# One packed array of per-partition constants in a retention, expert and feed-forward kernel

## The chip, the cores and the metric

The kernel runs on 1 core of one Trainium2 chip. Its time is device microseconds of one execution, the median over a few runs. The core's engines are TensorE (PE, its weight load PEld), VectorE (DVE), ScalarE (ACT), GpSimd (POOL) and SyncE (SP); a "q" behind an engine's name (SPq, ACTq) is its queue of DMA issues.

## The reference

Three layers follow each other. First a retention attention over 2 batches, 8 heads, 768 tokens and 64 features, in blocks, with a decay `lam` per head; then a mixture of 8 experts, one per token, chosen by gate logits with a bias that depends on the token's modality; then a feed-forward layer of width 2048.

```python
Dmask = np.where(rel >= 0, lam[:, None, None] ** rel[None, :, :], 0.0)
lam_pow = lam[:, None, None] ** (pos[None, :, None] + 1)
for b in range(nb):
    intra = np.einsum('bhic,bhjc->bhij', qb, kb) * Dmask[None]
    intra = np.einsum('bhij,bhjd->bhid', intra, vb)
    inter = np.einsum('bhid,bhde->bhie', qb * lam_pow[None], kv_state)
    out[:, :, sl] = intra + inter
    kv_state = lam_block * kv_state + np.einsum('bhsd,bhse->bhde', kb * rev_pow[None], vb)
...
logits = x @ w_gate + modality_bias[modality_id]
e_idx = np.argmax(logits, axis=1)
out[mask] = gate_w[mask, None] * (np.maximum(x[mask] @ w1[e], 0.0) @ w2[e])
...
h = x @ w_in
return (h * np.clip(h + 3.0, 0.0, 6.0) / 6.0) @ w_out
```

## The kernel before, in words

The work has three stages in time: the attention (to about 75 us), the experts (to about 230 us) and the feed-forward layer (to the end). The attention goes over 12 units of 128 tokens, alternating between the two batches. Each unit has four loads of 256 KB: q_t and k_t (`load`, L326) and k_n and v_n (`load_rows`, L336). The tiles have four buffers, so units 0 to 2 are loaded up front and unit u+3 in the loop.

Before the loads of units 0 and 1 are finished, small constants are loaded:

- `lam_bc` (L350): the 8 decays, the same on every partition, 32 bytes per partition, from ACT.
- `lam_p` (L353): for each of the two halves of the partitions, every second decay (4 numbers, with a step of 2 in memory), in two transfers from ACT.
- the gate columns (L360): `w_gate`, four runs of 8 numbers per partition, straight into the last 8 columns of `iw`, whose first 128 columns of each block are the identity; from SP.
- `bias_bc` (L362): the 16 modality biases on every partition; from SP.
- `mod_i` (L366): the modality of each token; from SP.

What uses them: DVE makes `dmask` from `lam_bc` with eight scans (L373), and in `late_constants` (L398) `qdec` from `lam_p` with four scans (L400), `m_f` from `mod_i` (L408), and `bias_tok` from `m_f` and `bias_bc` (L413 to L416). The matmuls of `rows` (L539, tile `xr`) multiply with `iw`, and so transpose a unit and compute its logits.

PE, ACT, DVE and SP run in the order in which the code is written; POOL's order is left to a scheduler. The order at the start is: 36 warm-up matmuls that use no input (L698, tile `warm`), `scores(0)` with its two mask products on DVE (L449, L451, tile `s_t`), `late_constants`, `decays(0)` on POOL and `key_decays(0)` on ACT (L459, L478, tile `k_d`), then for each unit the scores and mask products of the next unit, the state products (L499, tile `s_ps`) and the output products (L519, tile `o_ps`) of this one, and the `xr` matmuls of the unit before. So on DVE the mask products of unit 1 stand behind `qdec`, `m_f` and `bias_tok`. The second scores tile of unit 1 lies in the PSUM bank `xa` (L444), which the first `xr` tile (L537) uses next.

Each DMA from SP or ACT reports to one of eight semaphores (DMAHW0 to DMAHW7), in turn; a transfer waits until the one that used its semaphore eight transfers earlier has landed.

Of the kernel before, what the change touches and what calls it, by code (L numbers as in the profile page):

```python
# [11 lines left out]
F32 = mybir.dt.float32  # L12
# [11 lines left out]
P = 128  # L24
B, H, S, D = 2, 8, 768, 64
KA = 4
NPAIR = H // 2
# [5 lines left out]
KD = DM // P  # L33
E = 8
# [18 lines left out]


@with_exitstack
def retention_moe_ffn(ctx, tc, qT, kT, kn, vn, lam, mod, w_gate, bias, w1, w2, win, wout, out):
    nc = tc.nc
    ctx.enter_context(tc.manual_schedule(engines={ENG.PE, ENG.Activation, ENG.DVE, ENG.SP}))

# [253 lines left out]
    with ExitStack() as ac:  # L313
        acon = ac.enter_context(tc.tile_pool(name="acon", bufs=1))
# [11 lines left out]
        def load(u):  # L326
            b, c = units[u]
            i = b * NC + c
            q_t = ap.tile([P, NPAIR, C], F32, tag="q_t", name="q_t")
            k_t = ap.tile([P, NPAIR, C], F32, tag="k_t", name="k_t")  # L330
            v_n = ap.tile([P, DM], F32, tag="v_n", name="v_n")
            nc.sync.dma_start(out=q_t, in_=qT[i])
            nc.sync.dma_start(out=k_t, in_=kT[i])
            data[u] = (q_t, k_t, None, v_n)

        def load_rows(u):  # L336
            b, c = units[u]
            i = b * NC + c
            q_t, k_t, _, v_n = data[u]
            k_n = None  # L340
            if c < NC - 1:
                k_n = ap.tile([P, H, D], F32, tag="k_n", name="k_n")
                nc.sync.dma_start(out=k_n, in_=kn[i])
            nc.sync.dma_start(out=v_n, in_=vn[i])
            data[u] = (q_t, k_t, k_n, v_n)

        load(0)
        load(1)
        lam_bc = acon.tile([P, H], F32, name="lam_bc")
        nc.scalar.dma_start(out=lam_bc, in_=lam[0:1, :].broadcast_to([P, H]))  # L350
        lam_p = acon.tile([P, NPAIR], F32, name="lam_p")
        for t in range(2):
            nc.scalar.dma_start(  # L353
                out=lam_p[t * D:(t + 1) * D, :],
                in_=lam.rearrange("o (p t) -> o t p", t=2)[:, t, :].broadcast_to([D, NPAIR]),
            )
        load_rows(0)
        load_rows(1)
        iw = acon.tile([P, KD, P + E], F32, name="iw")
        nc.sync.dma_start(out=iw[:, :, P:], in_=w_gate.rearrange("(k p) e -> p k e", p=P))  # L360
        bias_bc = acon.tile([P, 2, E], F32, name="bias_bc")
        nc.sync.dma_start(  # L362
            out=bias_bc.rearrange("p m e -> p (m e)"),
            in_=bias.rearrange("m e -> (m e)").unsqueeze(0).broadcast_to([P, 2 * E]))
        mod_i = acon.tile([P, NTILE], I64, name="mod_i")
        nc.sync.dma_start(out=mod_i, in_=mod)  # L366

# [2 lines left out]
        for t in range(2):  # L370
            for p in range(NPAIR):
                h = 2 * p + t
                nc.vector.tensor_tensor_scan(  # L373
                    out=dmask[:, h, :], data0=lam_bc[:, h:h + 1].broadcast_to([P, C]), data1=ident,
# [12 lines left out]
            out=tri_bf, in_=ones_bf, pattern=[[1, P]], base=0, channel_multiplier=-1,  # L387
# [4 lines left out]
        iota(off_e, [[NT, E]])  # L392
        for k in range(KD):
            nc.gpsimd.tensor_copy(iw[:, k, :P], ident)
        qdec = acon.tile([P, NPAIR, C], F32, name="qdec")
        bias_tok = acon.tile([P, NC, B, E], F32, name="bias_tok")

# [421 lines left out]
    def picked(first, out):  # L819
# [7 lines left out]
            out=gt, in0=nrest.unsqueeze(2).broadcast_to([P, E, JMAX]), in1=thr, op=ALU.is_gt),  # L827
# [24 lines left out]
            out=posf, in0=ohs, in1=sxo.unsqueeze(1).broadcast_to([P, NTILE, E]), op=ALU.mult),  # L852
# [5 lines left out]
            out=to_a, in0=a_io[:, :NTILE].unsqueeze(1).broadcast_to([P, NTILE, NTILE]),  # L858
            in1=pos_a.unsqueeze(2).broadcast_to([P, NTILE, NTILE]), op=ALU.is_equal),
        lambda: V.tensor_tensor(  # L860
            out=to_ao, in0=to_a,
            in1=o_num.rearrange("p c b -> p (c b)").unsqueeze(2).broadcast_to([P, NTILE, NTILE]), op=ALU.mult),
        lambda: V.tensor_tensor(
            out=at_b, in0=b_io.unsqueeze(1).broadcast_to([P, NTILE, P]),
# [40 lines left out]
    with ExitStack() as fc:  # L905
# [52 lines left out]
        for n, (fb, tg, f) in enumerate(steps):  # L958
            m = n % (NTG * FB)
# [17 lines left out]
        for h in range(2):  # L977
            nc.vector.tensor_scalar(  # L978
                out=row2[:, h:h + 1], in0=row[:, i:i + 1], scalar1=2, scalar2=h, op0=ALU.mult, op1=ALU.add)
        ts = slice(TG - P, TG)  # L980
        for h in range(2):
# [3 lines left out]
            for f in range(FB):  # L985
# [6 lines left out]
                out=out.rearrange("n (h c) -> (n h) c", h=2),  # L992
                out_offset=bass.IndirectOffsetOnAxis(ap=row2[:, h:h + 1], axis=0),
                in_=acc[:, i, cs], in_offset=None), "out")


def _layout(inputs):
    f = {k: np.asarray(v) for k, v in inputs.items()}

    def feature_major(a):  # L1000
        a = a.reshape(B, NPAIR, 2, NC, C, D).transpose(0, 3, 2, 5, 1, 4)
        return np.ascontiguousarray(a).reshape(B * NC, P, NPAIR, C)

    def token_major(a):
        return np.ascontiguousarray(a.transpose(0, 2, 1, 3)).reshape(B * NC, C, DM)

    w1 = f["moe_w1"].reshape(E, KD, P, KF1 // 2, 2, P).transpose(0, 3, 2, 4, 1, 5)
    w2 = f["moe_w2"].reshape(E, KF1, P, KD, P).transpose(0, 3, 2, 1, 4)
    win = f["moe2_w_in"].reshape(KD, P, NFB, FB, P).transpose(2, 1, 3, 0, 4)
    wout = f["moe2_w_out"].reshape(NFB, FB, P, DM).transpose(0, 2, 1, 3)  # L1010
    return {
        "qT": feature_major(f["q"]),
        "kT": feature_major(f["k"]),
        "kn": token_major(f["k"]).reshape(B * NC, C, H, D),
        "vn": token_major(f["v"]),
        "lam": f["lam"].reshape(1, H),
        "mod": np.ascontiguousarray(f["moe_modality_id"].reshape(B, NC, P).transpose(2, 1, 0)).reshape(P, NTILE),
        "w_gate": f["moe_w_gate"],
        "bias": f["moe_modality_bias"],
        "w1": np.ascontiguousarray(w1).reshape(E, KF1 // 2, P, 1024),  # L1020
        "w2": np.ascontiguousarray(w2).reshape(E, KD, P, 1024),
        "win": np.ascontiguousarray(win).reshape(NFB, P, FB * DM).view(np.int64),
        "wout": np.ascontiguousarray(wout).reshape(NFB, P, FB * DM).view(np.int64),
    }
# [17 lines left out]
```

## Time and profile before

| what | us |
|---|---|
| median of 3 runs | 507.0 |
| lowest and highest run | 506.35, 510.4 |
| profiled execution, its own time | 509.76 |
| its span, first to last instruction | 507.8 |
| PE busy in the span | 483.7 |
| DVE, ACT, POOL busy | 315.1, 219.5, 71.6 |
| mean granted TensorE clock | 0.98 of full |

Busy times are those of one profiled execution, and its times below are microseconds from the first instruction. PE is busy 95% of the span, so a gain has to come from the rest or from matmuls that run at a lower clock.

### The profile page before, as it was taken

The page shows a single profiled execution, that of the slowest core. Times are in us where ns is not written, and L with a number is a line of the kernel's source. Part 1 is how long each engine was busy: PE and PEld are TensorE (multiplying, and loading weights), DVE is VectorE, ACT ScalarE, POOL GpSimd, SP SyncE. Part 2 cuts the span into 40 slices and gives each one's busy share as a digit, 9 for nine tenths or more (in the row PEclk, how much of TensorE's full clock was granted, in tenths as well). Part 3 has the DMA queues.
Part 4 walks back from the last instruction along what each step waited for, and adds up shares of the span by engine and source line. Part 5 has one row for each costly group of instructions (what it writes and reads, how often), then busy time and mean ns, then how long its engine had stood idle before and what let it go on. Part 6 is the DMA issues. An engine that isn't in the chain of part 4 may idle for free.

```text
span 507.8 us, 8695 instructions
## 1 busy us (share of the span) xinstructions
PE 483.7 (95%) x3322; PEld 424.1 (84%) x3322; DVE 315.1 (62%) x615; ACT 219.5 (43%) x405; POOL 71.6 (14%) x106
## 2 busy tenths in 40 slices
PE   5999999889999999996999999999999999999995
PEld 4878789789999999995888888888888888888885
DVE  4577789856888877661647445766556776424252
ACT  0555556356666565631453534343334334222230
POOL 3554351320303030000000000000000000003033
PEclk8899999989999999997999999999999999999998
DMA  4986463866868776602212211221203120002022
GB/s 137 370 275 198 159 240 129 243 176 215 267 227 265 233 221 196 229 25 87 80 46 83 62 63 43 83 79 46 83 16 110 43 83 1 0 0 84 0 84 83
DMA packets 25327, 64.29 MB, mean 127 GB/s; under 512 B 5954, under 2 KB 6053, under 8 KB 25277
## 3 DMA queue, kind: packets, MB, share of 16 engines
q1 hardware_dynamic: 22173, 57.25, 35.1%
q0 software_dynamic: 2416, 6.39, 3.8%
q8 instruction: 28, 0.46, 0.4%
q14 instruction: 22, 0.18, 0.1%
q10 hardware_dynamic: 688, 0.01, 0.1%
HBM read 57.29 MB, written 6.34 MB: 125 GB/s over the span
## 4 chain that ended last, share of the span: by engine, by line
PE 53%; POOL 0%; POOLq 0%; DVE 0%; issue 0%
PE ph L925 27%; PE po L944 26%; POOLq L1038 0%; POOL out_y L991 0%; POOL out_y L953 0%; DVE acc L951 0%; DVE row L978 0%
## 5 line engine op out<-in xcount | busy, mean ns | idle before, releaser
L930 DVE SCALAR_TENSOR_TENSOR g<-r,ph 128x512 f32<-128x512 f32 x48 | 33.0, 687 | 68.1 <-ACT r L928 68.1
L944 PE MATMUL po<-wo_hi,g_lo 128*128 128x512 f32 x188 | 74.0, 394 | 0.0
L944 PE MATMUL po<-wo_lo,g_hi 128*128 128x512 f32 x188 | 73.9, 393 | 0.0
L944 PE MATMUL po<-wo_hi,g_hi 128*128 128x512 f32 x188 | 73.1, 389 | 0.0
L928 ACT ACTIVATE r<-ph,half 128x512 f32<-128x512 f32 x48 | 33.0, 688 | 81.3 <-PE ph L925 81.3
L214 DVE TENSOR_TENSOR wlo<-wraw,whi 128x1024 fp32r<-128x1024 f32 x46 | 56.1, 1222 | 16.7 <-ACT whi L210 16.6
L925 PE MATMUL ph<-y_hi,wi_hi 128*128 128x512 f32 x192 | 53.6, 402 | 4.0 <-DVEq L886 4.0
L953 POOL DMA_INDIRECT out_y<-acc,row x11 | 10.7, 968 | 307.5 <-DVE acc L951 304.5
L925 PE MATMUL ph<-y_lo,wi_hi 128*128 128x512 f32 x192 | 53.9, 403 | 0.0
L934 DVE TENSOR_TENSOR g_lo<-g,g_hi 128x512 fp32r<-128x512 f32 x48 | 33.3, 693 | 33.0 <-ACT g_hi L932 33.0
L925 PE MATMUL ph<-y_hi,wi_lo 128*128 128x512 f32 x192 | 53.2, 399 | 0.0
L210 ACT CAST whi<-wraw 128x1024 fp32r<-128x1024 f32 x48 | 50.1, 1046 | 4.4 <-DMA wraw<-in_w 4.4
L925 PEld LDWEIGHTS ph<-y_hi,wi_hi 128*128 128x128 f32 x192 | 36.9, 193 | 12.4 <-ACTq L886 4.2
L932 ACT CAST g_hi<-g 128x512 fp32r<-128x512 f32 x48 | 29.8, 621 | 36.2 <-DVE g L930 36.2
L925 PEld LDWEIGHTS ph<-y_hi,wi_lo 128*128 128x128 f32 x192 | 36.9, 192 | 8.8
L925 PEld LDWEIGHTS ph<-y_lo,wi_hi 128*128 128x128 f32 x192 | 36.6, 191 | 8.8
L944 PEld LDWEIGHTS po<-wo_lo,g_hi 128*128 128x128 f32 x188 | 35.3, 188 | 8.6
L944 PEld LDWEIGHTS po<-wo_hi,g_hi 128*128 128x128 f32 x188 | 35.4, 188 | 8.4
L944 PEld LDWEIGHTS po<-wo_hi,g_lo 128*128 128x128 f32 x188 | 35.3, 188 | 7.5
L226 POOL DMA_INDIRECT xg<-x_d,ix x18 | 23.0, 1277 | 89.1 <-DMA ix<-order_d 59.6
L273 PE MATMUL ps<-x_hi,whi 128*128 128x264 f32 x192 | 31.9, 289 | 0.0
L273 PE MATMUL ps<-x_lo,whi 128*128 128x264 f32 x192 | 31.7, 288 | 0.0
(173 smaller groups left out, 796.9 us busy)
## 6 DMA issues: line engine op xcount, KB each, us to landing
wraw<-in_w SPq DMA_DIRECT2D x48, 512.0 KB, 3.7
raw<-in_win SPq DMA_DIRECT2D x16, 512.0 KB, 3.8
raw<-in_wout SPq DMA_DIRECT2D x16, 512.0 KB, 4.8
q_t<-in_qT SPq DMA_DIRECT2D x12, 256.0 KB, 4.5
k_t<-in_kT SPq DMA_DIRECT2D x12, 256.0 KB, 4.9
v_n<-in_vn SPq DMA_DIRECT2D x12, 256.0 KB, 5.6
x_d<-x_s SPq DMA_DIRECT2D x12, 256.0 KB, 2.3
k_n<-in_kn SPq DMA_DIRECT2D x10, 256.0 KB, 7.8
```

The costliest lines, as they stand in the source:

```text
L210: nc.scalar.copy(hi.rearrange("p a f -> p (a f)"), raw)
L214: (low or nc.vector).tensor_tensor(out=lo[:, js, :], in0=raw.rearrange("p (a f) -> p a f", f=P)[:, js, :], in1=hi.bitcast(F32)[:, js, :], ...
L226: ld = nc.gpsimd.indirect_dma_start(out=xg, out_offset=None, in_=x_d[0:EARLY * B * P, :] if s == LEAD else x_d[:], in_offset=bass.Indirect ...
L273: nc.tensor.matmul(ps, w[:, 4 * f2 + k, :], x[:, k, :], start=(m == 0), stop=(m == 3 * KD - 1))
L925: nc.tensor.matmul(ph, w[:, f, k, :], y[:, k, cols], start=(n == 0), stop=(n == 3 * KD - 1))
L928: nc.scalar.activation(r6, ph, ACTF.Relu, scale=1.0 / 6.0, bias=half)
L930: nc.vector.scalar_tensor_tensor(out=g, in0=r6, scalar=1.0, in1=ph, op0=ALU.min, op1=ALU.mult)
L932: nc.scalar.copy(g_hi, g)
L934: nc.vector.tensor_tensor(out=g_lo, in0=g, in1=g_hi.bitcast(F32), op=ALU.subtract)
L944: nc.tensor.matmul(pos_[t], g[:, ts], w[:, f, :], start=(f == 0 and n == 0), stop=(f == FB - 1 and n == 2))
L953: rows_apart(nc.gpsimd.indirect_dma_start(out=out, out_offset=bass.IndirectOffsetOnAxis(ap=row[:, i:i + 1], axis=0), in_=acc[:, i, :], in_ ...
```

## The change

The host lays lam (8 columns), the per-half lam (4), the gate columns (32) and the two bias rows (16) out as one array of 128 rows with 60 numbers, 240 bytes each. One transfer from ACT, where `lam_bc` was, loads it into the tile `cst`; `lam_bc`, `lam_p`, `gate_c` and `bias_bc` are slices of that tile. The gate columns come into `iw` by a copy on POOL.

```diff
-def retention_moe_ffn(ctx, tc, qT, kT, kn, vn, lam, mod, w_gate, bias, w1, w2, win, wout, out):
+def retention_moe_ffn(ctx, tc, qT, kT, kn, vn, small, mod, w1, w2, win, wout, out):
...
-        lam_bc = acon.tile([P, H], F32, name="lam_bc")
-        nc.scalar.dma_start(out=lam_bc, in_=lam[0:1, :].broadcast_to([P, H]))
-        lam_p = acon.tile([P, NPAIR], F32, name="lam_p")
-        for t in range(2):
-            nc.scalar.dma_start(
-                out=lam_p[t * D:(t + 1) * D, :],
-                in_=lam.rearrange("o (p t) -> o t p", t=2)[:, t, :].broadcast_to([D, NPAIR]),
-            )
+
+        cst = acon.tile([P, H + NPAIR + KD * E + 2 * E], F32, name="cst")
+        nc.scalar.dma_start(out=cst, in_=small)
+        lam_bc = cst[:, :H]
+        lam_p = cst[:, H:H + NPAIR]
+        gate_c = cst[:, H + NPAIR:H + NPAIR + KD * E].rearrange("p (k e) -> p k e", k=KD)
+        bias_bc = cst[:, H + NPAIR + KD * E:].rearrange("p (m e) -> p m e", m=2)
         load_rows(0)
         load_rows(1)
         iw = acon.tile([P, KD, P + E], F32, name="iw")
-        nc.sync.dma_start(out=iw[:, :, P:], in_=w_gate.rearrange("(k p) e -> p k e", p=P))
-        bias_bc = acon.tile([P, 2, E], F32, name="bias_bc")
-        nc.sync.dma_start(
-            out=bias_bc.rearrange("p m e -> p (m e)"),
-            in_=bias.rearrange("m e -> (m e)").unsqueeze(0).broadcast_to([P, 2 * E]))
         mod_i = acon.tile([P, NTILE], I64, name="mod_i")
         nc.sync.dma_start(out=mod_i, in_=mod)
...
         for k in range(KD):
             nc.gpsimd.tensor_copy(iw[:, k, :P], ident)
+        nc.gpsimd.tensor_copy(iw[:, :, P:], gate_c)
...
+    lam, gate = f["lam"], f["moe_w_gate"]
+    small = np.concatenate([
+        np.broadcast_to(lam, (P, H)),
+        np.repeat(lam.reshape(NPAIR, 2).T, D, axis=0),
+        gate.reshape(KD, P, E).transpose(1, 0, 2).reshape(P, KD * E),
+        np.broadcast_to(f["moe_modality_bias"].reshape(1, 2 * E), (P, 2 * E)),
+    ], axis=1)
```

SP's queue at the start, before, from the fifth transfer on, with the semaphore that each waits for (DMAHW0 is that of lam_bc, DMAHW1 of the first q_t, DMAHW2 and DMAHW4 of the two lam_p):

```order
L343 DMA k_n_142<-in_kn 128x512
L344 DMA v_n_129<-in_vn 128x512 [waits DMAHW0_49]
L343 DMA k_n_145<-in_kn 128x512 [waits DMAHW1_49]
L344 DMA v_n_134<-in_vn 128x512 [waits DMAHW2_49]
L360 DMA iw_148<-in_w_gate 128x4x8 [waits DMAHW3_49]
L362 DMA bias_bc_150<-in_bias 128x16 [waits DMAHW4_49]
L366 DMA mod_i_152<-in_mod 128x12 [waits DMAHW5_49]
L332 DMA q_t_190<-in_qT 128x512 [waits DMAHW6_49]
L333 DMA k_t_191<-in_kT 128x512 [waits DMAHW7_49]
```

The same place now (DMAHW0 is that of cst, DMAHW1 and DMAHW2 of the first q_t and k_t):

```order
L343 DMA k_n_139<-in_kn 128x512
L344 DMA v_n_129<-in_vn 128x512
L343 DMA k_n_142<-in_kn 128x512
L344 DMA v_n_134<-in_vn 128x512 [waits DMAHW0_49]
L360 DMA mod_i_146<-in_mod 128x12 [waits DMAHW1_49]
L332 DMA q_t_185<-in_qT 128x512 [waits DMAHW2_49]
L333 DMA k_t_186<-in_kT 128x512 [waits DMAHW3_49]
```

Two transfers are gone from SP and two from ACT, the rest keeps its order; two transfers that waited now wait for nothing, and the others wait for other transfers than before.

POOL at the start, the difference between before (-) and now (+), around the copies into `iw`:

```order
 L74 IOTA rev_e 128x8
 L74 IOTA off_e 128x8
-L394 COPY iw<-ident 128x128 [waits Pool_49]
-L386 AFFINE_SELECT tri_bf<-ones_bf 128x128 [waits Pool_49]
-L394 COPY iw<-ident 128x128 x3
-L417 MEMSET half 128x1
+L388 COPY iw<-ident 128x128 [waits Pool_49]
+L380 AFFINE_SELECT tri_bf<-ones_bf 128x128 [waits Pool_49]
+L388 COPY iw<-ident 128x128 x3
+L389 COPY iw<-cst 128x4x8 [waits DMAHW0_49]
+L412 MEMSET half 128x1
 L74 IOTA thr 128x48
```

The copy of the gate columns, which waits for cst, stands in front of `half` and the iotas of `late_constants`; apart from line numbers nothing else moved on POOL. The order on PE and DVE is the one of before.

## Rows read from the trace of the kernel before

**Rows 1.** The page: PE's busy tenths in 40 slices of the span.
```profile
PE   5999999889999999996999999999999999999995
```

**Rows 2.** Timeline of PE: start, us, instructions, [idle before, releaser].
```profile
6.73 0.61 PE L449 MATMUL sc<-q_t,k_t 64*128 64x128 f32 x7
11.77 2.08 PE L449 MATMUL sc<-q_t,k_t 64*128 64x128 f32 x16 [4.43 <-DMA k_t<-in_kT]
...
15.49 1.71 PE L519 MATMUL o_ps<-s_t,v_n 128*64 128x128 f32 x15
17.13 1.16 PE L449 MATMUL sc<-q_t,k_t 64*128 64x128 f32 x16
18.22 0.50 PE L539 MATMUL xr<-iw,x_t 128*128 128x136 f32 x2
```

**Rows 3.** Timeline of DVE, 4 to 18.5 us.
```profile
4.66 2.65 DVE L373 TENSOR_TENSOR_SCAN dmask<-lam_bc,ident 128x128 f32<-128x128 f32 x8 [4.66 <-DMA lam_bc<-in_lam]
7.37 1.29 DVE L451 TENSOR_TENSOR s_t<-sc,dmask 128x512 f32<-128x512 f32 x2
11.25 1.37 DVE L400 TENSOR_TENSOR_SCAN qdec<-lam_p,zrow 128x128 f32<-128x128 f32 x4 [2.59 <-DMA lam_p<-in_lam]
15.20 0.25 DVE L408 TENSOR_SCALAR m_f<-mod_i 128x12 f32<-128x12 int32 x2 [2.58 <-DMA mod_i<-in_mod]
...
15.87 0.74 DVE L416 TENSOR_TENSOR bias_tok<-bias_tok,b 128x96 f32<-128x96 f32 x1
16.54 1.27 DVE L451 TENSOR_TENSOR s_t<-sc,dmask 128x512 f32<-128x512 f32 x2
```

**Rows 4.** Timeline of POOL and ACT, up to 15 us.
```profile
5.22 0.29 POOL L429 TENSOR_SCALAR_AFFINE_SELECT below<-below 128x64 f32<-128x64 f32 x1
...
12.38 1.28 ACT L478 ACT_TABLE_LOAD   x1 [12.38 <-DMA k_n<-in_kn]
12.46 0.62 POOL L459 TENSOR_TENSOR k_d<-k_n,dmask 128x256 f32<-128x256 f32 x1 [6.95 <-DMA k_n<-in_kn]
...
13.68 1.06 ACT L478 ACTIVATE k_d<-k_n,dmask 128x64 f32<-128x64 f32 x4
```

**Rows 5.** Windows: length, PE PEld DVE ACT POOL busy (count), clock, DMA share, GB/s.
```profile
2.00:5.00 3.00, 3.00 (x30) 3.00 (x29) 0.34 (x1) 0.00 (x0) 3.00 (x16) 1.00 0.62 169
5.00:8.00 3.00, 2.34 (x25) 1.95 (x22) 2.94 (x10) 0.00 (x0) 0.43 (x3) 1.00 0.27 88
8.00:10.00 2.00, 0.00 (x0) 0.00 (x0) 0.66 (x2) 0.00 (x0) 0.00 (x0) 1.00 0.06 13
...
10.30:11.00 0.70, 0.00 (x0) 0.00 (x0) 0.00 (x0) 0.00 (x0) 0.00 (x0) 0.50 0.89 310
11.00:16.00 5.00, 4.00 (x39) 3.74 (x41) 2.13 (x9) 2.35 (x5) 1.47 (x3) 0.50 1.07 352
```

**Rows 6.** Timeline of the DMA issues of ACT and SP: start, us of issue.
```profile
1.26 0.42 SPq L333 DMA_DIRECT2D k_t<-in_kT  x1
1.27 1.40 ACTq L353 DMA_DIRECT2D lam_p<-in_lam  x2
...
1.73 0.42 SPq L332 DMA_DIRECT2D q_t<-in_qT  x1
...
2.20 0.55 SPq L333 DMA_DIRECT2D k_t<-in_kT  x1
...
7.77 0.51 SPq L360 DMA_DIRECT2D iw<-in_w_gate  x1
11.17 0.34 SPq L362 DMA_DIRECT2D bias_bc<-in_bias  x1
```

**Rows 7.** DMA queue of ACT, first 16 us: packets, MB, share of 16 engines.
```profile
q10 hardware_dynamic: 688, 0.01, 2.0%
```

**Rows 8.** SP's waits: us in total, times, longest.
```profile
SPq L362 <- DMA lam_p<-in_lam: 2.9, 1, 2.9
```

**Rows 9.** Windows, 20 to 25 us.
```profile
20.00:25.00 5.00, 5.00 (x82) 4.40 (x80) 2.12 (x6) 2.32 (x7) 4.81 (x9) 1.00 1.05 383
```

More of the change, by code (lines that the diff above doesn't have):

```diff
@@ L1015, in _layout @@
         "vn": token_major(f["v"]),
-        "lam": f["lam"].reshape(1, H),
+        "small": small,
         "mod": np.ascontiguousarray(f["moe_modality_id"].reshape(B, NC, P).transpose(2, 1, 0)).reshape(P, NTILE),
-        "w_gate": f["moe_w_gate"],
-        "bias": f["moe_modality_bias"],
         "w1": np.ascontiguousarray(w1).reshape(E, KF1 // 2, P, 1024),
```

## Prediction

> **What bounds the kernel now.** I read the page first, for where TensorE is not busy. Its 40 slices of 12.7 us show PE at 8 to 9 tenths almost everywhere; the first stands at 5, the last at 5 too, and one near the middle, between the expert stage and the last stage, at 6 [rows 1]. All that the change touches is loaded once, in that first slice, so the question is what ends last there, and whether time won there lasts to the end of the program.
>
> Next, the engines in the order of time. In the first 17 us each of them waits for a DMA: PE for k_t of unit 1 (4.43 us, until 11.77), DVE for lam_p and then for mod, ACT and POOL for k_n until 12.4 [rows 2 to 4]. The transfers were not short of bandwidth: the core moved 169 GB/s from 2 to 5 us, 88 from 5 to 8, 13 from 8 to 10, and 352 from 11 to 16 us [rows 5]. The loads stood still while most of the first eight were issued.
>
> Bytes against issue order tell what they stood behind. A load of q_t, k_t, k_n or v_n is 256 KB, 0.262 MB. From 2 to 5 us came 0.507 MB, nearly q_t and k_t of unit 0; from 5 to 8 us 0.264 MB, one load, q_t of unit 1; then almost nothing, and from 10.3 us the rest pours in [rows 5]. After the first q_t and lam_bc, the issues were k_t at 1.26, two lam_p from 1.27 on over 1.40 us, q_t at 1.73, k_t at 2.20 [rows 6]. So the slow stretches lie just where a lam_p stands. Each lam_p reads one number at a time: ACT's queue made 688 packets for 0.01 MB, 640 of them data (128 for lam_bc, 256 for each lam_p), the rest 16 completions for each of three transfers [rows 7]. Moreover SP's bias_bc, which reuses the second lam_p's semaphore, waits for it 2.9 us, until 11.17, and behind it stand mod and all loads of unit 2 [rows 6, 8].
>
> **The change, part by part.**
>
> Removed: three ACT transfers become one, and w_gate (0.51 us of issue) and bias_bc (0.34) leave SP's queue [rows 6]. In the new order v_n of unit 0 and k_n of unit 1 wait for nothing, v_n of unit 1 for cst, mod for the first q_t. Everything up to mod can be issued by about 5.5 us instead of after 11.5.
>
> The new array has 128 rows of 240 bytes and takes lam_bc's place in front. The trace has no such transfer; nearest is lam_bc, 128 rows of 32 bytes, for which DVE waits until 4.66 [rows 3]. Earlier gains nothing: the first mask products start at 7.37, when the first scores end too (6.73 + 0.61 = 7.34) [rows 2, 3]. The other end is a landing as late as the second lam_p's, 11.25. I take 4.66, since form and place are lam_bc's.
>
> When do the loads land? With no lam_p between them the six left at 5 us are 1.57 MB; at the 383 GB/s of a busy stretch [rows 9] they end at 9.1 us. From bytes to release cost about 0.5: k_t and k_n, the first 0.524 MB after 10.3, were through at 11.9 (0.217 MB by 11.0, 0.307 MB at 352 GB/s), and ACT went on at 12.38 [rows 4, 5]. So k_t of unit 1 is there by 6.9, k_n of unit 0 by 7.6, mod by 9.7. These are late bounds, as bytes will flow better before 5 us too.
>
> The Trainium skill ("DMA: Bandwidth & Descriptors", Queues, rings and completion order) says that each DMA engine takes the queue rows that have work in turn, packet by packet, and that SP and ACT each have a row of their own. By that rule lam_p in ACT's row would not hold up the loads in SP's, the standstill would have another cause, and the sum would be the 0.9 us of the first rival instead of 5.4. The order of the bytes speaks against it so far.
>
> The DVE chain now: first mask products 7.37 to 8.66, qdec only at 11.25 (lam_p), m_f only at 15.20 (mod), second mask products at 16.54 [rows 3]. New: qdec at 8.66, needing only cst, plus 1.37 is 10.03; mod is there, and from m_f to the second products it takes 16.54 - 15.20 = 1.34, so they start at 11.37 and end 1.27 later, at 12.64. The start moves by 5.17 us.
>
> The PE chain: the scores of unit 1 follow those of unit 0 at 7.34. In the gap of now the granted clock fell, and it stood at 0.50, the 1.2 GHz level, over 11 to 16 us [rows 5]; the same 16 matmuls took 2.08 us there and 1.16 later [rows 2]. Without the gap I count full clock, and scores to 8.5. ACT: table load at 7.6, 1.28, so k_d begins at 8.9. From k_d's start to the end of the output products of unit 0 it took 13.68 to 17.20 [rows 2, 4], 3.5 us; by the ratio of the clock 2.0, so to 10.9, and the scores of unit 2 to 12.1. Next in PE's order are the xr matmuls, at 18.22 now. They write the bank that the second mask products have to leave: 12.64, say 12.8. That is 5.4 us earlier.
>
> From there PE's order is the same as before, and PE was busy 5.00 of 5.00 us from 20 to 25, with the loads already coming freely [rows 9]; no DMA of the first loads ends a wait behind it. So the shift goes through to the end. POOL gets a wait: the copy of the gate columns stands for cst in front of its iotas. That list ends at 5.51 now (5.22 + 0.29); with 1.5 us of wait and 0.3 for the copy it ends at 7.3, and POOL's next work, k_d, comes after k_n at 7.6, so the wait is covered. Its price without that cover is the 1.8 us, on POOL alone. Should the iotas slow the scans beside them by a tenth of 2.65 us, that is 0.3 us; I charge nothing, since they run beside them until 5.51 now too [rows 3, 4].
>
> **Sum.** 5.4 us off the profiled execution: span 507.8 to 502.4, its time 509.76 (1.96 around the span) to 504.4. The median of the runs is 507.0, 2.76 below the profiled one; on that footing the forecast is 501.6. Ends: 6.1 us if the last bias sum, 0.74 in the chain between m_f and the second products [rows 3], cost nothing; 0.9 if the standstill stays.
>
> **Rivals.**
>
> *The standstill has another cause, and the loads still come at 10.3.* For: the packets of ACT's queue filled only 2.0% of the engines' first 16 us [rows 7]. Against: the byte count, which stops twice in just that order. Then five loads (1.31 MB) stand before mod: 0.217 MB by 11.0, the rest at 383 GB/s to 13.9, landed 14.4, second products at 15.7, 0.9 us gained: 506.1. The Trainium skill (the same page, Rules for kernel authors) holds that a transfer issued early and waited for late has its fixed cost hidden, which would leave nothing to win by merging small ones but their issue. The trace does not agree here: DVE stood 2.59 us for lam_p and 2.58 for mod [rows 3].
>
> *Half of it returns.* mod lands late (each us past 10.03 costs one), or PE's clock falls again in the short waits around 8.7 and 12.4 us. Price of the clock: the work from 12.8 to about 17 at half speed, some 3 us. Against: the fall now came with 4.4 us without any matmul, and the new gaps are under 1 us. Gain 2.4: 504.6.
>
> *Slower: cst is late.* One transfer of 30 KB now gates the masks, which needed 4 KB. From its landing to the second mask products stand 2.65 + 1.29 + 1.37 + 1.34 = 6.65 us [rows 3], so it costs time from a landing at 16.54 - 6.65 = 9.89 on. At lam_p's 11.25 the products start at 17.9, 1.4 later: 508.4. For: it carries 7.5 times the bytes. Against: lam_bc, in the same number of rows, was there at 4.66.
>
> **How the numbers follow.** Forecast (4.5 to 6.1 us gained) 0.70; standstill stays 0.12; half returns 0.13; slower 0.05. A change of 1% is 5.07 us, about what a measurement of this kernel can tell from none; the forecast lies only just beyond it, so of its 0.70 I put 0.49 past 1%, and 0.01 on a larger gain elsewhere: faster 0.50. The rest of it, the two middle cases and part of the last are within 1%: 0.47; slower by over 1% 0.03. The range runs from a gain of 6.1 us, less twice the 0.65 between the two lower runs of before, to the case of the standstill: 499.6 to 506.1.
>
> **What would show it.** Right: no stretch of a microsecond under 100 GB/s between 3 and 9 us; second scores at about 7.4; qdec at 8.7, m_f by 10.1, second mask products near 11.4, xr near 12.8; granted clock at 1.00 through the first slice. Wrong: a standstill before 10 us without any lam_p; masks that begin later than 5 us; an early xr with a span that is not shorter.

## The result, and the profile after

| what | before | after |
|---|---|---|
| median of 20 executions, us | 508.64 | 501.12 |
| ratio, with its 95% interval | | 0.9875 (0.9856 to 0.9894) |
| profiled execution, its own time | 509.76 | 502.03 |
| its span | 507.8 | 500.2 |
| PE busy in the span | 483.7 | 480.8 |

The change makes the kernel 1.25% faster, 5.4 to 7.3 us of 508.64 by the interval, which leaves two disturbed executions of after out. The page's slices show where; this is after, and its PE line and granted clock answer to [rows 1]:

```profile
PE   7999999899999999969999999999999999999995
PEclk9999999899999999997999999999999999999998
```

The first slice rises from 5 tenths to 7; the rest has the old pattern. The head in the timeline of after, in order of time (start, length, engine, line, what it makes from what, count, and in brackets the idle time before it with what ended it), against [rows 2 to 4]:

```profile
3.79 0.21 POOL L389 COPY iw<-cst 128x32 f32<-128x32 f32 x1 [0.61 <-DMA cst<-in_small]
3.83 2.65 DVE L367 TENSOR_TENSOR_SCAN dmask<-cst,ident 128x128 f32<-128x128 f32 x8 [3.83 <-DMA cst<-in_small]
...
5.68 2.06 PE L444 MATMUL sc<-q_t,k_t 64*128 64x128 f32 x32
6.03 0.54 POOL L424 TENSOR_SCALAR_AFFINE_SELECT below<-below 128x64 f32<-128x64 f32 x1
6.88 1.29 DVE L446 TENSOR_TENSOR s_t<-sc,dmask 128x512 f32<-128x512 f32 x2 [0.39 <-PE sc L444]
...
7.79 1.28 ACT L473 ACT_TABLE_LOAD   x1 [7.79 <-DMA k_n<-in_kn]
7.86 0.62 POOL L454 TENSOR_TENSOR k_d<-k_n,dmask 128x256 f32<-128x256 f32 x1 [1.29 <-DMA k_n<-in_kn]
8.08 2.01 DVE L395 TENSOR_TENSOR_SCAN qdec<-cst,zrow 128x128 f32<-128x128 f32 x4
9.09 1.06 ACT L473 ACTIVATE k_d<-k_n,dmask 128x64 f32<-128x64 f32 x4
9.49 1.22 PE L494 MATMUL s_ps<-v_n,k_d 128*64 128x64 f32 x15 [1.75 <-ACT k_d L473]
...
10.01 0.22 DVE L403 TENSOR_SCALAR m_f<-mod_i 128x12 f32<-128x12 int32 x2
...
11.39 1.27 DVE L446 TENSOR_TENSOR s_t<-sc,dmask 128x512 f32<-128x512 f32 x2
...
11.57 1.16 PE L444 MATMUL sc<-q_t,k_t 64*128 64x128 f32 x16
...
12.81 1.17 PE L534 MATMUL xr<-iw,x_t 128*128 128x136 f32 x8
```

The waits of DVE for lam_p and mod are gone: neither the qdec nor the m_f row has a bracket, so nothing held them but the instruction ahead. PE's wait for k_t is gone too, the scores of units 0 and 1 stand in one row of 32. The first xr begins at 12.81 instead of 18.22, 5.41 us earlier, and the last one of the attention at 67.71 instead of 73.09, 5.38 earlier: what was won in the head is still there 55 us later. The last xr rows, of before and of after:

```profile
73.09 1.13 PE L539 MATMUL xr<-iw,x_t 128*128 128x136 f32 x8
```

```profile
67.71 1.12 PE L534 MATMUL xr<-iw,x_t 128*128 128x136 f32 x8
```

In the windows of after (length; busy time of PE, PEld, DVE, ACT, POOL with counts; granted clock, DMA share, GB/s) the loads flow without a stop, where [rows 5] had 169, 88 and 13 GB/s:

```profile
2.00:5.00 3.00, 3.00 (x30) 3.00 (x29) 1.17 (x4) 0.00 (x0) 2.39 (x14) 1.00 1.00 346
5.00:8.00 3.00, 2.74 (x41) 2.44 (x38) 2.61 (x7) 0.21 (x1) 1.63 (x8) 1.00 0.99 343
8.00:10.00 2.00, 0.51 (x5) 0.42 (x5) 2.00 (x5) 1.99 (x5) 1.18 (x2) 1.00 1.03 387
```

**The other 2.2 us of the profiles.** The spans differ by 7.6 us, the first xr by 5.4. The rest appears in the expert stage, around the first wait of PE for gathered rows: instruction by instruction PE's lead is still 5.4 us at the `rw` matmuls (99.17 and 93.78 us) and 7.4 about 10 us later. PE's timeline there, first of before, then of after:

```profile
99.48 1.23 PE L296 MATMUL py<-h_hi,whi 128*128 128x264 f32 x8
...
104.15 0.96 PE L240 MATMUL xt<-ident,xg 88*128 88x88 f32 x8 [2.17 <-DMA xg<-x_d,ix]
```

```profile
94.09 1.98 PE L296 MATMUL py<-h_hi,whi 128*128 128x264 f32 x8
...
97.63 1.56 PE L240 MATMUL xt<-ident,xg 88*128 88x88 f32 x12
```

Before ran the py matmuls at full speed, then stood 2.17 us for the gathered rows xg, and had the low clock after that (0.66 from 105 to 110 us). After had the low clock at once (1.98 instead of 1.23 for eight), and so never waited for xg. This differs from profile to profile: from the first xr to the end of the span it is 489.6 us before, 487.4 after, 487.9 in a second profile of after, and between 484.8 and 490.0 over all twelve profiles, whatever was edited in the head. It goes with the granted clock there: the four profiles in which it stays at 1.00 from 90 to 110 us (e2, e3, e5, e10) have 484.8 to 487.0 us, the eight with a mean of 0.83 to 0.91 in that stretch 487.4 to 490.0. Two of the four carry the full standstill in the head (e2, e3), so this isn't the change's doing as far as these profiles show. No run isolates it, and I count it to the spread and not to the change.

### The profile page after: what moved, and what is told of

The parts are those of the page before. It is cut to its first block, busy times and chain, and to the rows that moved or that the text cites. A ratio compares the mean times of both kernels' runs of the same rounds, so it can differ in the third digit from the quotient of the medians.

```text
span 500.2 us, 8690 instructions
## 1 busy us (share of the span) xinstructions
PE 480.8 (96%) x3322; PEld 421.6 (84%) x3322; DVE 315.0 (63%) x615; ACT 219.3 (44%) x405; POOL 71.3 (14%) x107
## 4 chain that ended last, share of the span: by engine, by line
PE 53%; POOL 0%; POOLq 0%; issue 0%; DVE 0%
PE ph L920 27%; PE po L939 26%; POOLq L1038 0%; POOL out_y L986 0%; POOL out_y L948 0%; DVE acc L946 0%; DVE row L973 0%
```

## The experiments

All of them but after_again edit the head. Two times sum up each: the landing of k_n of unit 0, read from the start of ACT's table load (which waits for it, but not in e6 and e9), and the start of the first xr. Each is read from a single profile. The ratio is against before, run beside it on the same chip. A hot transfer is one whose packets all read the same 32 bytes.

| kernel | k_n | first xr | median us | ratio (95%) |
|---|---|---|---|---|
| before | 12.38 | 18.22 | 507.6 to 508.6 | |
| after | 7.79 | 12.81 | 501.12 | 0.9875 (0.9856 to 0.9894) |
| after_again | 7.21 | 12.74 | 501.16 | 0.9862 (0.9840 to 0.9885) |
| e1 lam_p alone | 8.23 | 13.63 | 502.96 | 0.9899 (0.9856 to 0.9942) |
| e2 gate and bias alone | 12.58 | 18.72 | 507.58 | 0.9989 (0.9962 to 1.0016) |
| e3 two hot transfers added | 11.87 | 17.64 | 508.67 | 1.0008 (0.9980 to 1.0037) |
| e4 hot, whole rows | 8.12 | 13.31 | 503.23 | 0.9898 (0.9848 to 0.9948) |
| e5 single numbers, own rows | 8.03 | 13.48 | 500.29, one run | |
| e8 one hot transfer added | 10.23 | 16.19 | 506.06, one run | |
| e10 before, lam_p from own rows | 8.26 | 14.13 | 503.03 | 0.9897 (0.9839 to 0.9956) |
| e6 order and table | | 11.74 | 503.04 | 0.9894 (0.9864 to 0.9923) |
| e9 order spread | | 11.79 | 502.02 | 0.9866 (0.9816 to 0.9915) |

### Which half carries the gain: e1 and e2

e1 is before, with only lam_p read from an array that the host laid out, in one transfer instead of two, one run of 16 bytes per partition:

```diff
-        for t in range(2):
-            nc.scalar.dma_start(
-                out=lam_p[t * D:(t + 1) * D, :],
-                in_=lam.rearrange("o (p t) -> o t p", t=2)[:, t, :].broadcast_to([D, NPAIR]),
-            )
+        nc.scalar.dma_start(out=lam_p, in_=lamp)
```

e2 is after, with lam_bc and the two lam_p read as in before, and only the gate columns and the bias taken from `cst`.

> Before, with lam_p alone read from a contiguous array (one transfer, 128 rows of 16 bytes, instead of two of 256 single numbers); lam_bc, gate and bias as before. If the single-number packets hold up SP's loads: no standstill after 3 us, the second mask products start at 11.4 to 12, xr at 12.8 to 13.5, and the time falls by 4.5 to 5.5 us (ratio to before about 0.990). If the standstill has another cause (gate and bias in SP's queue, or the start itself): the loads come at 10.3 as before, gain 1 us at most.

> The other half: gate and bias from one packed transfer (ACT, behind lam_p), lam_bc and the two lam_p read as before. If the single-number packets hold up the loads: standstill as before until about 10 us, xr at 16.5 to 18, gain 0 to 1.5 us (ratio 0.997 to 1.000). If gate and bias were the cause: loads flow, gain 4 us or more.

e1 has the first xr at 13.63, so 4.59 of the 5.41 us, and nearly all of the time (0.9899, 0.9856 to 0.9942). e2 has the old standstill, the xr 0.5 us later than before, and no gain (0.9989, 0.9962 to 1.0016). The gain is lam_p's; merging gate and bias alone, with lam_p as it was, is worth nothing that can be measured. The 0.8 us that e1 lacks lie in its slower start: the loads move at 108 and 147 GB/s from 3 to 5 us, while lam_bc still reads one row for all partitions and SP waits 1.3 us for it, and mod, behind gate and bias, is issued at 7.30 instead of 4.57, so that m_f waits 0.47 us. No run separates these two. Windows of e1, then of e2:

```profile
3.00:4.00 1.00, 1.00 (x12) 1.00 (x11) 0.00 (x0) 0.00 (x0) 1.00 (x7) 1.00 0.64 108
4.00:5.00 1.00, 1.00 (x15) 1.00 (x13) 0.00 (x0) 0.00 (x0) 1.00 (x7) 1.00 0.68 147
5.00:6.00 1.00, 0.36 (x7) 0.18 (x4) 0.99 (x4) 0.00 (x0) 0.44 (x3) 1.00 1.05 369
```

```profile
5.00:6.00 1.00, 1.00 (x11) 0.80 (x10) 1.00 (x5) 0.00 (x0) 0.00 (x0) 1.00 0.05 0
...
8.00:9.00 1.00, 0.00 (x0) 0.00 (x0) 0.99 (x2) 0.00 (x0) 0.00 (x0) 1.00 0.02 0
```

### What in lam_p: e3, e4, e5, e8 and e10

e3, e4, e5 and e8 are after, with transfers behind `cst` on ACT that fill a tile which nothing reads. e3 repeats the form of lam_p; the others change the source, or the count:

```diff
         nc.scalar.dma_start(out=cst, in_=small)
+        spare = acon.tile([P, NPAIR], F32, name="spare")
+        for t in range(2):
+            nc.scalar.dma_start(out=spare[t * D:(t + 1) * D, :], in_=...)
# e3: single numbers, all partitions from row 0 (e8: the same with range(1))
+  small[0:1, :H].rearrange("o (p t) -> o t p", t=2)[:, t, :].broadcast_to([D, NPAIR])
# e4: one run of 16 bytes per partition, all from row 0
+  small[0:1, H:H + NPAIR].broadcast_to([D, NPAIR])
# e5: single numbers, each partition from its own row
+  small[t * D:(t + 1) * D, :H].rearrange("q (p t) -> q t p", t=2)[:, t, :]
```

> After, plus two transfers like the old lam_p (64 partitions, 4 numbers with a step of 2, all from one row) behind cst on ACT, into a tile that nothing reads. If their packets hold up the loads: two stretches under 100 GB/s between 4 and 10 us, k_n of unit 0 lands at about 12, xr at 16 to 18 though no engine waits for the extra tile, and 3.5 to 5 us of the gain are lost (ratio to before 0.995 to 1.000). If the gain came only from waits for small transfers' semaphores: like e4. If neither: as after.

> Control for e3: after, plus two transfers behind cst on ACT to the same tile, from the same row and on the same semaphores, but 64 contiguous runs of 16 bytes each instead of 256 single numbers. If the number of packets counts: 128 extra packets instead of 512, loads delayed by a quarter of e3's standstill at most, xr by 13.5, time within 0.7 us of after. If the reused semaphores or the one hot row count: as slow as e3.

> Like e3 (after, plus two transfers of 256 single numbers), but every partition reads from a row of its own, 240 bytes apart, instead of all from one row. If the number of packets holds up the loads: standstill as in e3, k_n of unit 0 lands near 12, xr near 17.6. If it is the one row that all read: loads flow, xr near 13.

> After, plus one such transfer (64 partitions, 256 single numbers) instead of e3's two. If each transfer costs its own standstill: one slow stretch, k_n of unit 0 near 10 (between 7.8 of after and 11.9 of e3), xr near 15. If only the second counted, because it stood in front of the second unit's k_t: as e3 or as after.

e3 loses the whole gain (1.0008, 0.9980 to 1.0037) although nothing waits for its tile: two such transfers are enough. e5 sends the same 512 single numbers, from rows of their own, and the first loads are delayed by 0.24 us only. The DMA view from 4 to 8 us shows it best (all packets with their MB; then per queue packets, MB and the time of the packets as a share of 16 engines; q1 is SP's, q10 ACT's). First e3, then e5:

```profile
DMA packets 593, 0.39 MB, mean 98 GB/s; under 512 B 403, under 2 KB 403, under 8 KB 593
...
q1 hardware_dynamic: 209, 0.39, 35.0%
q10 hardware_dynamic: 384, 0.00, 4.4%
```

```profile
DMA packets 1077, 1.30 MB, mean 324 GB/s; under 512 B 445, under 2 KB 445, under 8 KB 1077
...
q1 hardware_dynamic: 707, 1.29, 95.2%
q10 hardware_dynamic: 370, 0.00, 5.2%
```

ACT's queue did the same in both: 384 and 370 packets in 4.4% and 5.2% of the engines' time. SP's queue moved 0.39 MB in the one and 1.29 in the other. SP had its first five loads, 1.31 MB, issued before 4 us in e3 as well (k_n at 2.77), so this is no lack of issues. In e3 the engines spent about 60% of these 4 us on no packet that the records show. So the standstill is not the price of 512 packets as such, nor of their own time: it comes when all of them read the same 32 bytes. The branch of e5's expectation by which the number of packets decides is refuted.

The shared semaphores are not the cause either. SP waits for the two extra transfers in e5 and e4 too (1.3 and 0.9 us, 0.6 and 0.9), as in e3 (1.5 and 2.3), without a standstill like e3's. They probably set the 0.67 us that e5's first xr is behind after's: its scores of unit 2 wait 0.52 us for k_t, which SP issues at 8.13 us, behind the second of these waits, instead of 5.52.

e8, with one hot transfer, lies between. The row that waits for k_n, in the timelines of e8, e3 and e5 in turn, against 7.79 in after:

```profile
10.23 1.28 ACT L476 ACT_TABLE_LOAD   x1 [10.23 <-DMA k_n<-in_kn]
```

```profile
11.87 1.28 ACT L476 ACT_TABLE_LOAD   x1 [11.87 <-DMA k_n<-in_kn]
```

```profile
8.03 1.28 ACT L476 ACT_TABLE_LOAD   x1 [8.03 <-DMA k_n<-in_kn]
```

256 hot packets cost 2.4 us, 512 cost 4.1; since after_again has its k_n at 7.21, each of these is good to some 0.6 us, and e5's 0.24 is no difference. e8's first xr, at 16.19, came later than the 15 expected: PE stood 3.12 us for k_t, and its clock then fell (0.50 from 12 to 14 us).

e4 has 128 packets on one row and costs the first xr 0.5 us; its loads dip to 193 and 119 GB/s from 4 to 6 us and then go on at 367. Its windows:

```profile
4.00:5.00 1.00, 1.00 (x12) 1.00 (x10) 1.00 (x4) 0.00 (x0) 1.00 (x8) 1.00 0.80 193
5.00:6.00 1.00, 1.00 (x11) 0.80 (x10) 1.00 (x4) 0.00 (x0) 0.95 (x6) 1.00 0.49 119
```

Taken alone, e4 answers its expectation with the number of packets, and against the one row. Together with e5 it says that both count: many packets, and all on one row. Which part the size of a read has is not settled, since e4 has fewer packets and longer ones, and 512 whole-row reads of one row were not tried. e4's time (four runs, 501.99 to 504.47) lies 2.1 us above after's where at most 0.7 was expected, but its interval holds both.

e10 is the counter-test in before itself: lam_p stays two transfers of 256 single numbers, lam_bc, gate and bias stay, but each partition reads lam_p from a copy of lam in a row of its own:

```diff
-                in_=lam.rearrange("o (p t) -> o t p", t=2)[:, t, :].broadcast_to([D, NPAIR]),
+                in_=lamr[t * D:(t + 1) * D, :H].rearrange("q (p t) -> q t p", t=2)[:, t, :],
...
+        "lamr": np.broadcast_to(np.tile(f["lam"], 8), (P, 64)),
```

> Before, with the two lam_p transfers still of 256 single numbers each, but every partition reads its own row of a 256-byte-per-partition array instead of all the same 32 bytes; the rest as before. If the one row that all read holds up the loads (e5 against e3): no standstill after 5 us, xr by 14, gain 4 to 5.5 us (ratio 0.989 to 0.992), as in e1. If the number of packets does: as before.

The page counts 688 packets in ACT's queue, as in before, and the standstill is gone: k_n at 8.26, the first xr at 14.13, 4.1 us of the 5.4, and a ratio of 0.9897 (0.9839 to 0.9956). Windows of e10:

```profile
4.00:5.00 1.00, 1.00 (x12) 1.00 (x10) 0.00 (x0) 0.00 (x0) 1.00 (x7) 1.00 0.51 151
5.00:6.00 1.00, 0.87 (x9) 0.60 (x6) 0.82 (x3) 0.00 (x0) 0.61 (x3) 1.00 1.07 343
6.00:7.00 1.00, 0.92 (x14) 0.95 (x16) 1.00 (x4) 0.00 (x0) 0.00 (x0) 1.00 1.11 359
8.00:9.00 1.00, 0.80 (x15) 0.61 (x12) 1.00 (x3) 0.74 (x1) 0.62 (x1) 1.00 1.04 383
```

One microsecond of e10, from 10 to 11, is still at 102 GB/s, and no run explains it. In e1, e2 and e10 the first xr came 0.1 to 0.7 us later than the latest time expected (13.5, 18 and 14), which changes none of these answers.

### Whether more can be won in the head: after_again, e6 and e9

e6 is after with a one-element activation on ACT at the very start, which takes the table load before k_n lands, and with `qdec`, `m_f` and `bias_tok` moved behind the second mask products on DVE. e9 has the same table load, but spreads these constants: `qdec` after the state copy of unit 0, `m_f` and `bias_tok` after the mask products of unit 2. after_again is the changed kernel, unedited, beside them.

```diff
+        pre = acon.tile([P, 1], F32, name="pre")
+        nc.vector.memset(pre, 1.0)
+        nc.scalar.activation(pre, pre, ACTF.Copy, scale=1.0)
         load_rows(0)
...
+                if u == 0:
+                    scores(1)
+                    vector_constants()
+                    decays(1)
...
# e9 instead:
+                if u == 1:
+                    bias_constants()
...
+            if u == 0:
+                vector_constants()
```

> After once more, as the measure for e6 and a second profile: xr at 12.8 again; ratio to before 0.986 to 0.990. Between the first xr and the last instruction before took 489.6 us and after 487.4 in their profiles; if that difference is by chance (how long PE waits for the first gather and when its clock falls there), this profile may lie anywhere from 486.5 to 489.7; if it belongs to the change, it is 487.4 again.

> After, with what now ends last in the head taken away: DVE makes the second mask products before qdec, m_f and bias_tok, and ACT loads its table at the start with a one-element activation instead of after k_n of unit 0. If the DVE order and the table load are what xr waits for: second mask products at about 8.2, k_d at 7.9, xr at 11.4 to 11.7 and 1.1 to 1.4 us less than after (ratio to before lower by 0.002 to 0.003). If k_n's landing alone sets the head: no change.

> After, with the early table load of e6 and DVE's late constants spread: the second mask products right after the first, qdec after the copy of unit 0's state, m_f and bias_tok after the mask products of unit 2. In e6 the gain of 1.0 us at the first xr was gone at the second xr (16.51 against 16.42), since the state products of unit 1 waited for the state copy behind bias_tok on DVE. If that is all: xr of unit 0 at 11.7 and of unit 1 near 15.5 (16.4 in after), about 1 us less than after, ratio to before 0.984 to 0.987. If the head is bound otherwise: second xr at 16.4 and no gain.

e6 starts the first xr 1.0 us earlier and has lost it at the second: 16.51, against 16.42 in after_again, because the state copy of unit 0 (tile `s_new`) now stands behind `bias_tok` on DVE. Its timeline:

```profile
11.74 1.19 PE L542 MATMUL xr<-iw,x_t 128*128 128x136 f32 x8
...
12.82 0.67 DVE L417 TENSOR_TENSOR bias_tok<-bias_tok,b 128x96 f32<-128x96 f32 x1
13.41 0.41 DVE L508 COPY s_new<-s_ps 128x256 f32<-128x256 f32 x1
...
16.51 1.19 PE L542 MATMUL xr<-iw,x_t 128*128 128x136 f32 x8
```

e9, where that copy stands in front again, shows that this was the reason: its second xr begins a microsecond earlier.

```profile
15.50 1.19 PE L543 MATMUL xr<-iw,x_t 128*128 128x136 f32 x8
```

e9 keeps the microsecond through the attention (last xr at 66.69, against 67.64 in after_again), but the time doesn't show it: 0.9866 (0.9816 to 0.9915) beside 0.9862 (0.9840 to 0.9885) and 0.9875 (0.9856 to 0.9894). One microsecond is 0.2%, and the interval reaches 0.5% to each side. e6's ratio, 0.9894, is no better than that of after_again. No version tried is shown to beat the changed kernel.

## Why the prediction was right, and where it was not

**Path and terms.** The second mask products were forecast for 11.37 and began at 11.39; m_f for 10.03, began at 10.01; the first xr for 12.8, began at 12.81; the table load for 7.6, began at 7.79; the clock stayed at 1.00 from 2 to 16 us. No microsecond between 3 and 9 us had less than 318 GB/s. The step from the first xr to the end, "the shift goes through", holds for the whole attention (5.38 of 5.41 at the last xr). One reading was too small: PE's new gap, put at under 1 us, was 1.75 before the first s_ps, and the clock stayed up all the same.

**Steps that came out right by two errors.** DVE began qdec at 8.08, not 8.66, since the first scores ended earlier; and it took 2.01 us instead of 1.37. The two nearly cancel. On PE the work from k_d to the end of the output products was put at 2.0 us and took 11.57 - 9.09 = 2.48. The forecast scaled all of it with PE's clock, but ACT's four pieces of k_d, which feed it, take 1.06 us in both profiles. This cost nothing: the scores of unit 2, behind this work, end at 12.73, and the second mask products, the bound that the forecast used, at 12.66.

**The edits costed at nothing.** `cst` landed at 3.8, before the 4.66 of lam_bc, and as forecast this gained little: its masks were done at 6.48, and the products waited 0.39 us for the scores. POOL's copy of the gate columns was covered, its iotas ended at 6.57 and k_n came at 7.86. e2 shows that the two SP transfers gain nothing while lam_p is as before.

**The size.** The sum of 5.4 us is the lower end of the measured 5.4 to 7.3. That the forecast of 501.6 lies 0.5 us from the median is partly luck. It was put on the three runs' median of 507.0; over 20 executions before is at 508.64, and 5.4 less is 503.2. So the level was 1.6 us too low, and the gain that the medians show 2.1 us above the sum; these two errors nearly cancel. Part of the second can be read from the executions of one kernel, which differ by their mean granted clock: after took 499.0 to 501.1 us in the eleven at 0.992 to 0.996, and 501.3 to 503.9 in the seven at 0.983 to 0.987. Before shows the same two groups at 0.983 to 0.989 (506.0 to 508.0 us) and 0.977 to 0.980 (508.1 to 510.6), counted in the nineteen beside e1. Median against median of these groups the gain is 6.0 us (506.4 to 500.4) and 6.5 (509.4 to 503.0), nearer to the sum than the 7.5 of the medians. Matching the groups is an argument from order: the lower clock of before's two is put down to the head, where 0.50 from 10.3 to 16 us in [rows 5] is 5.7 x 0.5 / 507.8 = 0.006 of the mean. The clock in the expert stage, by which the profiles differ, is a candidate for what puts an execution into one group or the other; no run tests it, and it stays open, as does what is left between the sum and the gain.

**The cause, which was named too coarsely.** The prediction said of the standstill that "each lam_p reads one number at a time", and pointed to 640 data packets. That lam_p was the cause is shown (e1, e3). That the single numbers by themselves are the cause is refuted: e5 and e10 send as many, and the loads flow. What stops them is that all 256 packets of a transfer read one row of 32 bytes. The Trainium skill ("DMA: Bandwidth & Descriptors", Rules for kernel authors) says that a source that isn't contiguous in its last dimension becomes one descriptor per element. The packet counts agree (688 with two such transfers, 144 without), but the count alone does not make the price here. Had the source been changed and the count kept, as in e10, the prediction's reasoning would have expected no gain, and 4.1 us would have been there.

**The rivals.** That the standstill has another cause than lam_p is refuted: with it alone removed (e1) it goes, with it alone added (e3) it comes back. The other rule of the Trainium skill (the same page, Queues, rings and completion order), by which each DMA engine takes the rows of ACT and SP in turn, was the ground for the rival: read as if ACT's row could not hold up SP's. e3 shows that it can: SP's queue fell to 0.39 MB in 4 us while ACT's packets filled 4.4% of the time. The rule may still hold packet by packet; what fails is the reading that few and short packets therefore cost the other row little. That `cst` comes late, and that mod or the clock takes half back, did not occur.

Why many reads of one row hold up everything else, in the memory or in the DMA engines, no run here tells: the records show only no packet on the engines for most of that time (some 60% in e3).

## What to carry to other kernels

Don't fill the partitions from one small row in DRAM while large loads are on their way: let the host repeat it, one row per partition, or at least keep the reads of that row few (128 reads put the first xr back by 0.5 us here, 512 by 4.8). Look for it in the windows of a microsecond: low GB/s with a low DMA share while issued loads are still out, beside a small transfer whose packets take almost no time themselves. Check whether a gain in the head lasts at the end of the stage (here the last xr), not at its first instruction: after's 5.4 us lasted, and e6's microsecond was gone at the second xr.

## What the runs showed that was not expected

- **A hot row.** 256 reads of single numbers from the same 32 bytes delay the loads of another queue by 2.4 us (e8), 512 by 4.1 (e3); 512 from separate rows by 0.24 (e5), less than two profiles of after differ. 128 reads of whole runs from one row cost 0.5 us at the first xr (e4).
- **DVE's scans beside POOL.** qdec, four scans, takes 1.36 to 1.37 us where POOL does little or nothing beside it (before, e2, e3, e6, e8, e9), and 1.74 to 2.13 where 0.7 to 1.2 us of POOL's k_d run at the same time (after, after_again, e1, e4, e5, e10). In after 1.1 us of k_d lie beside it, and it takes 2.01. No run was made to isolate this; it is a pattern over twelve profiles. The forecast had charged nothing for POOL beside DVE.
- **The low clock wanders.** In the expert stage the stretch at the low clock comes before the first gather in one profile (0.73 from 95 to 100 us, after), behind it in another (0.66 from 105 to 110, before), and in four not at all. PE's wait for the gather differs too, from 0 to 2.4 us. Two microseconds between two single profiles can't be put down to an edit in the head unless they stand there already at the last xr.
